# Sparse attention, a routed expert layer and a second expert layer in one kernel: a front in another order, a placement step in bf16, two weight chunks ahead instead of three, and row transposes spaced by VectorE's backlog

## The chip, the core and the metric

The kernel runs on one core of a Trainium2 chip. The metric is the device time of one execution in microseconds, from start to end of the program. A profiled execution also has a span, the time from its first to its last instruction. TensorE (PE in the profile) does the matmuls and transposes, VectorE (DVE), ScalarE (ACT) and GpSimd (POOL) the elementwise work, and SyncE (SP) and GpSimd start the DMA transfers.

## What is computed

```python
# q, k, v: (4, 8, 576, 64); heads 0-3 attend locally (0 <= i-j < 32), heads 4-7 with stride 32
scores = scale * q @ k.T;  attn = softmax(where(mask, scores, -1e9));  attn_out = attn @ v
x = attn_out.transpose(0, 2, 1, 3).reshape(2304, 512)
# first layer: 8 experts (512 -> 1024 -> 512), at most 288 tokens each
logits = x @ w_gate;  order = argsort(-logits.flatten())   # greedy assignment in this order
for e in range(8):  out[assigned == e] = relu(x[assigned == e] @ w1[e]) @ w2[e]
# second layer: 4 experts, all tokens, weighted by p = domain_probs / sum
out2 = sum(p[:, e:e+1] * (relu(out @ v1[e]) @ v2[e]) for e in range(4))
```

## The kernel before, in words

The whole program is one instruction stream for each engine, written in Python in the order in which each engine runs it. An engine waits at an instruction until its operands are there, and everything behind it on that engine waits with it.

**The front** (`front`) does the attention of the four batches. A batch is 10 units: five strided units (two groups of 6 or 7 row pairs, heads 4 to 7) and then five local ones (heads 0 to 3). The loop over `t` is a software pipeline. In step `t` unit `t` gets its scores (`scores`, L186 strided and L189 local, with the mask and row minimum on VectorE, L196), unit `t-1` its exponentials on ScalarE (`exps`, L205), unit `t-2` its division on GpSimd (`norm`, L215), unit `t-4` the transposes of its probabilities (`tr_p`, L222, copied to `pT`), and unit `t-5` the product with v (`av`, L235 or L242, copied to `hold`). Beside these, each of eight steps of a batch (`t` mod 10 from 6 to 9 and from 0 to 3) prepares two of the 16 pieces of q and k of the next batch (`pre` calls `piece`). Four strided pieces each of q and k are four transposes of 72 columns (L153). Four local pieces each of q and k are six matmuls with the identity, each of 64 output rows and 96 columns, which the trace shows as 12 instructions (L164). A piece's copy out of PSUM goes to ScalarE or VectorE: `copy` gives "q" pieces to the two in turn by a counter of all copies, strided k pieces to ScalarE and local k pieces to VectorE. Batch 0's pieces are done ahead of the loop (the first eight) and in its first steps.

Loads of q, k and v are issued on SP's queue: for batch `b+2` q and k, and for batch `b+1` v, in step 2 of batch `b`. The strided part of v (`vs`) is 13 transfers a batch, of 18 to 126 rows of 512 bytes. Local q and k (`ql`, `kl`) come in pieces of 1536 contiguous bytes, the local part of v (`vl`) in pieces of 256.

**Routing and the first expert.** Behind the last unit, `search` finds the first expert's tokens, and `place` turns them into a list of row numbers: 18 bf16 matmuls (L708) give a small table `tk`, copied to f32, and three f32 matmuls of it with `rad` (L714, six instructions in the trace, as each f32 matmul is two) give `idx`. GpSimd gathers the rows of x by `idx` (`xg`, L902, three indirect DMAs), PE transposes them (L926), ScalarE and VectorE split them into high and low halves (`xh`, `xl`), and the first expert's matmuls (`l1`, L982) begin. Meanwhile `PRE` = 3 chunks of expert weights are loaded and split (a chunk is two transfers `raw` of 256 KB on SP, L829 and L830; the cast `wh` on ScalarE, L855; the rest `wl` on VectorE or GpSimd). PE runs `WAIT` = 16 matmuls on constants (L1329) while it waits for the rows.

**The experts.** PE then runs the chunks of both layers. Each product is three matmuls (high by high, high by low, low by high). The search, placement and gather of expert `g+1` are two generators that hand out work between the matmuls. `Pace` keeps a running estimate of PE's and VectorE's time in the program's order (`nc.pe`, `nc.dve`), and a `yield` says when the generator goes on. For experts 1 to 7 the gathered rows are transposed in four groups of three (L919), each into the one PSUM buffer `pb`; a group can start only when the split of the group before has been read out of it (`xh` on ScalarE, then `xl` on VectorE). The groups stand 1.8 us of the estimate apart.

Of the kernel before, what the change touches and what calls it, by code (L numbers as in the profile page):

```python
# [18 lines left out]
FT = mybir.dt.float32  # L19
# [10 lines left out]
WARM = 10  # L30
WAIT = 16
BUSY = (0, 8, 2)
MORE = (1, 1, 5, 1, 1, 1, 1, 1)

def dap(t, off, *dims):
    return bass.AP(tensor=t.tensor, offset=t.offset + off, ap=[list(d) for d in dims])

def front(tc, ident, hot, q, k, v, wg, dp, xd, L, ready, hold, deferred):
# [3 lines left out]
    with ExitStack() as st:  # L42
# [8 lines left out]
        def load_qk(b, kinds="sl"):  # L51
            T = LD.setdefault(b, {})
            if "s" in kinds:
                for nm in ("qs", "ks"):
                    T[nm] = ld.tile([72, 32, 64], FT, name=nm)
            n = 8 if b == 0 else 32
            for r in range(0, 32 if "s" in kinds else 0, n):
                for nm, src in (("qs", q), ("ks", k)):
                    nc.sync.dma_start(T[nm][:, r:r + n].rearrange("p r d -> p (r d)"), dap(src, (b * H + 4) * hs + r * D, [hs, 4], [32 * D, 18], [1, n * D]))
            for nm, src in (("ql", q), ("kl", k)) if "l" in kinds else ():  # L60
                T[nm] = ld.tile([96, 4, 6, 64], FT, name=nm)
                nc.sync.dma_start(T[nm].rearrange("p h r d -> p h (r d)"), dap(src, b * H * hs, [6 * D, 96], [hs, 4], [1, 6 * D]))

        def load_v(b, lo=0, hi=10):
            T = LD[b]
            if not lo:
                T["vs"] = ld.tile([126, 10, 128], FT, name="vs")
            for t, (b0, n) in list(enumerate(zip(starts, sizes)))[lo:hi]:
                p = 0
                while p < n:  # L70
                    h, rp = divmod(b0 + p, 16)
                    m = min(n - p, 16 - rp)
                    nc.sync.dma_start(T["vs"][18 * p:18 * (p + m), t], dap(v, (b * H + 4 + h) * hs + 2 * rp * D, [2 * D, m], [32 * D, 18], [1, 2 * D]))
                    p += m
# [11 lines left out]
        load_qk(1, "s")  # L86
        load_v(0, 6)
        load_qk(1, "l")
        load_vl(0)
        zero = cst.tile([128, 128], FT, name="zero")  # L90
# [51 lines left out]
        def piece(b, i):  # L142
# [12 lines left out]
            else:  # L155
# [5 lines left out]
                src, dst = LD[b][("ql", "kl")[j]], (QL, KL)[j][b]  # L161
                for t in range(3):
                    for x in range(2):
                        nc.tensor.matmul(p[64 * x:64 * x + 64, 96 * t:96 * t + 96], src[:, 2 * hp + x, 3 * a + t, :], ident[:96, :96], start=True, stop=True)  # L164
                copy(dst[:, hp, 32 * j:].rearrange("p (s a t) -> p a t s", a=2, t=3)[:, a], p[:, :288].rearrange("p (t s) -> p t s", t=3), sc, "q" if sc else "r")

# [207 lines left out]
        for t in range(N + 14):  # L374
            t_now[0] = t
            if t < N and t % 10 == 2 and units[t][0] + 1 < B:
                if units[t][0] + 2 < B:
                    load_qk(units[t][0] + 2)
                load_v(units[t][0] + 1)
                nxt = [(units[t][0] + 1, i) for i in ORDER]  # L380

# [16 lines left out]
            def at(d, f):  # L398
                if 0 <= t - d < N:
                    f(t - d)  # L400
# [21 lines left out]
            while late:  # L422
                late.pop(0)()
            if t == N + 4:
                logits(N - 1)
            at(5, av)
            rows("o")
            if t < N:
                at(10, logits)
            elif t == N + 3:  # L430
                logits(N - 3)
            elif t == N + 5:
                logits_local(N - 1)
            pre()
            at(1, exps)
            rows("s")
            if t < N:
                scores(t)
            pre()
        for x in late2 + late:  # L440
# [15 lines left out]
def route_consts(nc, cst):  # L456
    K = {}
# [49 lines left out]
    nc.gpsimd.affine_select(rsel, radix, pattern=[[-2, 3], [-6, 3], [-1, 2]], base=0, channel_multiplier=1, compare_op=OP.is_equal, fill=0.0)  # L507
    K["rad"] = cst.tile([128, 3, 3], FT, name="rad")
    nc.vector.tensor_reduce(K["rad"], rsel, AX.X, OP.add)
    K["first"] = [cst.tile([128, NC], FT, name="m0"), cst.tile([128, NC], FT, name="mw0"), cst.tile([128, NC + 3, 32], BF, name="oh0"),  # L510
# [173 lines left out]
def place(nc, K, wk, ps, out):  # L684
# [8 lines left out]
    if "W" not in K:  # L693
        K["W"] = wk.tile([128, NC * 18 + 110], BF, name="W")
        nc.gpsimd.memset(K["W"][:, NC * 18:], 0.0)
        K["tk"] = wk.tile([128, 224], FT, name="tk")
        nc.gpsimd.memset(K["tk"], 0.0)
# [32 lines left out]
HI = 2.0  # L730
PRE = 3

# [28 lines left out]
def experts(tc, ident, hot, K, L, xd, side, w1, w2, v1, v2, out, hold, deferred):  # L761
    nc = Pace(tc.nc)
    D, F = 512, 1024
    with ExitStack() as st:
# [126 lines left out]
        def chain_b():  # L891
            nt = 0
            for g in range(8):
# [21 lines left out]
                if g:  # L915
                    for dc in range(4):
                        p = ps.tile([128, 3, 96], FT, name="pb")
                        for k in range(3):
                            nc.tensor.transpose(p[:, k], xg[:, k, cs(dc)], ident[:96, :96])  # L919
                        split(X[0][:, dc], X[1][:, dc], p.rearrange("p k s -> p (k s)"), False)  # L920
                        yield 1.8
                else:
# [396 lines left out]

        loads(1, 3)  # L1320
        until(lambda: "gather" in R[0])
# [74 lines left out]
```

## Time and profile before

| | |
|---|---|
| time, median of 3 runs | 1187.33 us (1186.92 to 1189.51) |
| profiled execution | 1188.98 us, span 1187.3 us |
| PE busy | 1160.4 us, 98% of the span |
| DVE, ACT, POOL busy | 840.5, 618.6, 412.2 us |
| front, first score matmul to the last units | 12 to 124 us of the span |
| search and placement of the first expert | 124 to 146 us |
| first expert matmul | 154.5 us |

Busy time of PE counts overlapping and pipelined matmuls, so a stretch that is 98% busy can still hold work that takes longer than it must. The clock granted to TensorE is 1.00 when it runs at 2.4 GHz and 0.50 at 1.2 GHz.

### The profile page before, as it was taken

How to read it: one execution, taken by the hardware profiler on the slowest of the kernel's cores; microseconds unless marked ns; L12 is line 12 of the kernel's file. 1: busy time of each engine (PE TensorE's matmuls, PEld its weight loads, DVE VectorE, ACT ScalarE, POOL GpSimd, SP SyncE). 2: the span in 40 equal slices, each digit the busy share in tenths (PEclk: the TensorE clock that was granted, in tenths of full speed). 3: DMA queues.
4: the chain of work that ended last, by engine and by line, in shares of the span. 5: the costliest groups of instructions: out<-in, count | busy, mean ns of one | idle time of the engine just before them, and what ended most of it. 6: DMA issues, size and time to landing. Idle time of an engine off the chain costs nothing.

```text
span 1187.3 us, 24963 instructions
## 1 busy us (share of the span) xinstructions
PE 1160.4 (98%) x9088; PEld 1038.2 (87%) x9095; DVE 840.5 (71%) x2249; ACT 618.6 (52%) x1602; POOL 412.2 (35%) x456
## 2 busy tenths in 40 slices
PE   9999799999999999999999999999999999999997
PEld 5777588898898988899999999999898999899996
DVE  6777687787785877878765577777777776766663
ACT  5899455442442442555545455555555555555552
POOL 4333030000010001001012566565666556766553
PEclk9999899999999999999999999999999999999999
DMA  8772574553353442566665433333433333433320
GB/s 181 170 172 44 151 222 145 178 169 102 90 163 91 134 154 58 160 213 185 191 199 158 128 107 91 105 104 95 140 100 96 107 94 102 142 92 105 102 77 36
DMA packets 191955, 152.98 MB, mean 129 GB/s; under 512 B 27640, under 2 KB 158776, under 8 KB 191400
## 3 DMA queue, kind: packets, MB, share of 16 engines
q1 hardware_dynamic: 188664, 141.74, 41.1%
q0 software_dynamic: 3168, 9.65, 2.6%
q8 instruction: 71, 1.16, 0.4%
q14 instruction: 52, 0.43, 0.1%
HBM read 141.77 MB, written 9.58 MB: 127 GB/s over the span
## 4 chain that ended last, share of the span: by engine, by line
PE 83%; DVE 5%; DMA 4%; issue 3%; POOL 3%; ACT 2%; SPq 0%; POOLq 0%; DVEq 0%; ACTq 0%
PE o L982 36%; PE h L982 17%; PE h L1214 9%; PE pa L1214 7%; DMA raw<-in_moe_w_dram 3%; PE pb L1214 3%; PE tr L164 2%; DVE wl L757 2%; PE pt L222 2%; POOL wl L1201 1%; PE av L242 1%; PE s L186 1%; PE pa L608 1%; PE tr L153 1%; PE av L235 1%
## 5 line engine op out<-in xcount | busy, mean ns | idle before, releaser
L757 DVE TENSOR_TENSOR wl<-raw,wh 128x512 fp32r<-128x512 f32 x352 | 269.2, 795 | 5.5 <-ACT wh L855 2.2
L875 ACT ACTIVATE hh<-h 128x256 fp32r<-128x256 f32 (+1 forms) x256 | 100.1, 391 | 273.4 <-PE h L982 201.4
L982 PE MATMUL o<-wh,hh 128*128 128x512 f32 x576 | 227.1, 394 | 0.4 <-DVE hold L757 0.4
L982 PE MATMUL o<-wl,hh 128*128 128x512 f32 x576 | 226.9, 394 | 0.0
L982 PE MATMUL o<-wh,hl 128*128 128x512 f32 x576 | 225.9, 392 | 0.0
L855 ACT CAST wh<-raw 128x512 fp32r<-128x512 f32 x272 | 160.4, 619 | 68.6 <-DMA raw<-in_moe_w_dram 67.0
L757 DVE SCALAR_TENSOR_TENSOR hl<-h,hh 128x256 fp32r<-128x256 f32 (+1 forms) x256 | 110.0, 430 | 118.0 <-ACT hh L875 117.4
L1201 POOL TENSOR_TENSOR wl<-raw,wh 128x512 fp32r<-128x512 f32 x96 | 122.3, 1295 | 197.1 <-ACT wh L1200 165.4
L902 POOL DMA_INDIRECT xg<-xd,idx x24 | 26.4, 1101 | 352.7 <-DVE idx L757 281.4
L982 PEld LDWEIGHTS o<-wh,hl 128*128 128x128 f32 x576 | 108.3, 188 | 22.8
L982 PEld LDWEIGHTS o<-wh,hh 128*128 128x128 f32 x576 | 108.3, 188 | 6.2 <-PE h L982 0.6
L982 PEld LDWEIGHTS o<-wl,hh 128*128 128x128 f32 x576 | 108.4, 188 | 5.5
L757 DVE TENSOR_TENSOR wl<-sums,wh 128x512 fp32r<-128x512 f32 x96 | 81.7, 852 | 29.0 <-ACT wh L1187 28.9
L1187 ACT CAST wh<-sums 128x512 fp32r<-128x512 f32 x96 | 59.7, 623 | 81.4 <-POOL sums L1175 57.8
L982 PE MATMUL h<-xh,wh 128*128 128x288 f32 x256 | 76.3, 298 | 0.0
L982 PE MATMUL h<-xl,wh 128*128 128x288 f32 x256 | 76.0, 297 | 0.0
L982 PE MATMUL o<-hh,wl 128*128 128x288 f32 x256 | 75.9, 297 | 0.0
L982 PE MATMUL o<-hl,wh 128*128 128x288 f32 x256 | 75.8, 296 | 0.0
L982 PE MATMUL o<-hh,wh 128*128 128x288 f32 x256 | 75.8, 296 | 0.0
L982 PE MATMUL h<-xh,wl 128*128 128x288 f32 x256 | 75.6, 295 | 0.0
L982 PE MATMUL h<-y256l,wh 128*128 128x256 f32 x256 | 73.0, 285 | 0.2 <-DVE y256l L757 0.2
L982 PE MATMUL h<-y256h,wl 128*128 128x256 f32 x256 | 73.2, 286 | 0.0
(312 smaller groups left out, 2937.3 us busy)
## 6 DMA issues: line engine op xcount, KB each, us to landing
raw<-in_moe_w_dram SPq DMA_DIRECT2D x464, 256.0 KB
vl<-in_v_dram SPq DMA_DIRECT2D x16, 192.0 KB
ql<-in_q_dram SPq DMA_DIRECT2D x4, 576.0 KB
kl<-in_k_dram SPq DMA_DIRECT2D x4, 576.0 KB
qs<-in_q_dram SPq DMA_DIRECT2D x3, 576.0 KB
ks<-in_k_dram SPq DMA_DIRECT2D x3, 576.0 KB
xd<-y SPq DMA_DIRECT2D x2, 576.0 KB
xd<-hl SPq DMA_DIRECT2D x5, 192.0 KB
```

What stands on the lines that cost most here:

```text
L153: nc.tensor.transpose(p[:, 72 * a:72 * a + 72], src[:, r:r + 2, :].rearrange("p r d -> p (r d)"), ident[:72, :72])
L164: nc.tensor.matmul(p[64 * x:64 * x + 64, 96 * t:96 * t + 96], src[:, 2 * hp + x, 3 * a + t, :], ident[:96, :96], start=True, stop=True)
L186: nc.tensor.matmul(out[:rows], lt, rt, start=True, stop=True)
L222: nc.tensor.transpose(p[:keys, rows * j:rows * j + rows], T["p"][:rows, j, :keys], ident[:rows, :rows])
L757: return f(*args, **kw)
L855: nc.scalar.copy(c["h"][:, sl], c["raw"][a])
L875: nc.scalar.activation(hi, src, AF.Relu)
L902: nc.gpsimd.indirect_dma_start(out=xg[:, k, :], out_offset=None, in_=xd, in_offset=bass.IndirectOffsetOnAxis(ap=idx[:, k:k + 1], axis=0))
L982: nc.tensor.matmul(out, a, b, start=start, stop=stop)
L1187: nc.scalar.copy(S["W"][nm][0], src[nm]())
L1201: nc.gpsimd.tensor_tensor(l, r, h.bitcast(FT), OP.subtract)
L1214: mmx = lambda o, a, b, first, lastm, n: (nc.tensor.matmul(o, a, b, start=first, stop=lastm, skip_group_check=True), tick(n / 2315 + 0.009))
```

## The change

The change does these things, beside two constants:

- In the front, local q and k of batches 1 to 3 come with the four heads side by side (8 transfers a batch in place of 2, pieces of 256 bytes in place of 1536), so that a piece is three transposes of 128 rows and 96 columns in place of six matmuls (12 instructions). The copy of a local piece walks the same elements in another order: three neighbours at a time.
- Inside a step, the two pieces and the exponentials come first, then `logits` and `av`, and the scores last.
- For batches 1 to 3 the last five of the ten `vs` tiles (six transfers a batch) are issued on GpSimd. Loads are put in another order, and batch 1's strided q and k come in two halves.
- `rad` and `tk` are bf16, so that each product of L714 is one bf16 matmul.
- `PRE` is 2 and `WAIT` 13.
- For experts 1 to 7, the groups of row transposes stand as far apart as VectorE's estimated backlog and 0.6 us, at least 1.8 us.

```diff
-WAIT = 16
+WAIT = 13
...
             for nm, src in (("ql", q), ("kl", k)) if "l" in kinds else ():
...
+                T[nm] = ld.tile([96, 6, 4, 64], FT, name=nm)
+                for h in range(4):
+                    nc.sync.dma_start(T[nm][:, :, h, :], dap(src, (b * H + h) * hs, [6 * D, 96], [D, 6], [1, D]))
...
-                    nc.sync.dma_start(T["vs"][18 * p:18 * (p + m), t], dap(v, (b * H + 4 + h) * hs + 2 * rp * D, [2 * D, m], [32 * D, 18], [1, 2 * D]))
+                    (nc.gpsimd if b and t > 4 else nc.sync).dma_start(T["vs"][18 * p:18 * (p + m), t], dap(v, (b * H + 4 + h) * hs + 2 * rp * D, [2 * D, m], [32 * D, 18], [1, 2 * D]))
...
                 for t in range(3):
+                    if b:
+                        nc.tensor.transpose(p[:, 96 * t:96 * t + 96], src[:, 3 * a + t, 2 * hp:2 * hp + 2, :].rearrange("p h d -> p (h d)"), ident[:96, :96])
+                        continue
                     for x in range(2):
                         nc.tensor.matmul(p[64 * x:64 * x + 64, 96 * t:96 * t + 96], src[:, 2 * hp + x, 3 * a + t, :], ident[:96, :96], start=True, stop=True)
-                copy(dst[:, hp, 32 * j:].rearrange("p (s a t) -> p a t s", a=2, t=3)[:, a], p[:, :288].rearrange("p (t s) -> p t s", t=3), sc, "q" if sc else "r")
+                copy(dst[:, hp, 32 * j:].rearrange("p (s a t) -> p a s t", a=2, t=3)[:, a], p[:, :288].rearrange("p (t s) -> p s t", t=3), sc, "q" if sc else "r")
...
-            if t == N + 4:
-                logits(N - 1)
-            at(5, av)
             rows("o")
+            pre()
+            at(1, exps)
+            rows("s")
+            pre()
             if t < N:
                 at(10, logits)
...
-            pre()
-            at(1, exps)
-            rows("s")
+            at(5, av)
             if t < N:
                 scores(t)
-            pre()
...
-        K["tk"] = wk.tile([128, 224], FT, name="tk")
+        K["tk"] = wk.tile([128, 224], BF, name="tk")
...
-PRE = 3
+PRE = 2
...
                         split(X[0][:, dc], X[1][:, dc], p.rearrange("p k s -> p (k s)"), False)
-                        yield 1.8
+                        yield max(1.8, nc.dve + 0.6 - nc.pe)
```

The rows below are the instructions of an engine in the order in which it runs them, before and with the change. The change has more lines of code, so that its line numbers are higher by 5 to 12: L222 is L230 in it, L164 is L169, L215 is L223, L829 is L841.

PE at the start of batch 2 (step `t` = 20; `tr` is the PSUM tile of a piece, `s` of scores, `av` of the product with v), before:

```order
L222 MATMUL pt<-ident,pr 96x128 x4
L340 MATMUL xr<-four,lg 128x16
L345 MATMUL xr<-four,lg 32x16
L242 MATMUL av<-pT,vl 64x64 x8
L164 MATMUL tr<-ident,ql 64x96 x6
L186 MATMUL s<-kS,qS 126x126 x4
L164 MATMUL tr<-ident,ql 64x96 x6
```

The same step with the change:

```order
L230 MATMUL pt<-ident,pr 96x128 x4
L348 MATMUL xr<-four,lg 128x16
L353 MATMUL xr<-four,lg 32x16
L169 MATMUL tr<-ident,ql 128x96 x6
L250 MATMUL av<-pT,vl 64x64 x8
L194 MATMUL s<-kS,qS 126x126 x4
```

Two groups of six matmuls on either side of the scores have become one group of six transposes (two pieces of three) ahead of `av`.

GpSimd around the turn from the local units of batch 0 to the strided ones of batch 1 (`pr` are probabilities divided by their sums, in place), before:

```order
L215 TENSOR_TENSOR pr<-pr,r 128x4x96 x4
L215 TENSOR_TENSOR pr<-pr,r 128x2x96
L160 MEMSET kL 128x2x32
L215 TENSOR_TENSOR pr<-pr,r 126x4x126 x2
L215 TENSOR_TENSOR pr<-pr,r 108x4x108 x2
```

With the change:

```order
L223 TENSOR_TENSOR pr<-pr,r 128x4x96 x4
L223 TENSOR_TENSOR pr<-pr,r 128x2x96
L165 MEMSET kL 128x2x32
L78 DMA vs<-in_v_dram 108x1x128 x2
L78 DMA vs<-in_v_dram 36x1x128
L78 DMA vs<-in_v_dram 72x1x128
L78 DMA vs<-in_v_dram 108x1x128 x2
L223 TENSOR_TENSOR pr<-pr,r 126x4x126 x2
```

Six transfers of `vs` now stand between the division of the last local unit and that of the first strided unit, here and at the same place of batch 1; those for batch 1 stand ahead of the first division of all.

SP at the first expert (`raw` are weights, `side` takes a copy of the gathered rows' last columns and so waits for the gather), before:

```order
L843 TENSOR_LOAD ei_2625
L843 ISA x2
L829 ISA
L829 DMA raw<-in_moe_w_dram 128x4x128
L830 ISA
L830 DMA raw<-in_moe_w_dram 128x512
L829 ISA
L829 DMA raw<-in_moe_w_dram 128x4x128
L830 ISA
L830 DMA raw<-in_moe_w_dram 128x512
L829 ISA
L829 DMA raw<-in_moe_w_dram 128x4x128
```

With the change, from the second chunk on:

```order
L841 DMA raw<-in_moe_w_dram 128x4x128
L842 ISA
L842 DMA raw<-in_moe_w_dram 128x512
L918 DMA side<-xg 96x3x8
L841 ISA
L841 DMA raw<-in_moe_w_dram 128x4x128
L842 ISA
L842 DMA raw<-in_moe_w_dram 128x512
```

The third chunk's two loads now stand behind `side`. On ScalarE, before and then with the change (`hh` is the high half of the first matmuls' result, read out of PSUM):

```order
L855 CAST wh<-raw 128x512 x6
L879 CAST xh<-o 128x288 x4
L875 ACTIVATE hh<-h 128x288
L855 CAST wh<-raw 128x512 x2
L875 ACTIVATE hh<-h 128x288
```

```order
L867 CAST wh<-raw 128x512 x4
L891 CAST xh<-o 128x288 x4
L867 CAST wh<-raw 128x512 x2
L887 ACTIVATE hh<-h 128x288
L867 CAST wh<-raw 128x512 x2
```

The casts of the third chunk stand behind the rows' casts and ahead of the first `hh`.

## Rows read from the trace of the kernel before

**Rows 1.** The page, part 1: busy time, share of the span and instructions of each engine.

```profile
PE 1160.4 (98%) x9088; PEld 1038.2 (87%) x9095; DVE 840.5 (71%) x2249; ACT 618.6 (52%) x1602; POOL 412.2 (35%) x456
```

**Rows 2.** Busy time by stretch: length; PE, PEld, DVE, ACT, POOL; clock, DMA share, GB/s.

```profile
34.97:49.30 14.33, 14.33 (x222) 11.10 (x223) 10.35 (x51) 11.57 (x52) 4.06 (x6) 1.00 0.81 187
51.18:63.78 12.60, 12.60 (x206) 9.63 (x205) 10.36 (x72) 11.67 (x55) 4.88 (x7) 1.00 0.81 190
63.78:75.64 11.86, 11.86 (x214) 9.87 (x212) 9.08 (x53) 10.34 (x46) 3.75 (x5) 1.00 0.73 172
...
89.43:101.18 11.75, 11.75 (x213) 9.76 (x211) 9.27 (x53) 11.28 (x51) 4.15 (x6) 1.00 0.53 105
...
141.40:151.60 10.20, 7.52 (x38) 3.86 (x39) 5.42 (x19) 3.09 (x5) 4.20 (x4) 0.50 0.76 230
...
98.00:100.00 2.00, 2.00 (x44) 1.58 (x43) 1.18 (x11) 2.00 (x11) 0.75 (x2) 1.00 1.15 162
```

**Rows 3.** The chain that ended last, 64 to 92 us: start, length, what.

```profile
65.30 0.50 PE tr L164 x12
...
66.43 0.65 PE tr L164 x12
...
80.42 0.40 PE tr L153 x4
```

**Rows 4.** Groups of ScalarE instructions up to 125 us: busy time, mean ns, idle before.

```profile
L136 ACT ACTIVATE qL<-tr 128x288 f32<-128x288 f32 x7 | 4.8, 684 | 4.4 <-PE tr L164 4.2
...
L136 ACT ACTIVATE qS<-tr 128x288 f32<-128x288 f32 x11 | 4.5, 413 | 6.5 <-PE tr L153 6.3
```

**Rows 5.** All engines in order of time, 64 to 77 us: start, length, instruction, [idle, releaser].

```profile
71.72 1.29 POOL L215 TENSOR_TENSOR pr<-pr,r 126x504 f32<-126x504 f32 x1 [2.74 <-ACT hold L134]
...
75.64 0.65 PE L222 MATMUL pt<-ident,pr 126*126 126x126 f32 x4
```

**Rows 6.** GpSimd in order of time, 0 to 140 us.

```profile
10.66 0.57 POOL L119 DMA_DIRECT2D dpr<-in_moe_domain_probs_dram  x1
...
86.51 1.23 POOL L393 DMA_DIRECT2D xd<-side  x1 [1.85 <-DVE r L214]
```

**Rows 7.** All engines in order of time, 140 to 160 us.

```profile
143.38 0.45 SPq L829 DMA_DIRECT2D raw<-in_moe_w_dram  x1
...
144.86 1.44 PE L714 MATMUL pb<-rad,tk 128*128 128x3 f32 x6 [0.34 <-DVE tk L757]
...
146.34 0.16 DVE L757 CAST idx<-pb 96x3 int32<-96x3 f32 x1 [1.53 <-PE pb L714]
...
146.44 1.28 ACT L855 CAST wh<-raw 128x512 fp32r<-128x512 f32 x2 [7.33 <-DMA raw<-in_moe_w_dram]
...
154.07 0.38 SPq L829 DMA_DIRECT2D raw<-in_moe_w_dram  x1
...
154.51 0.48 PE L982 MATMUL h<-xh,wh 128*128 128x288 f32 x1
...
156.55 0.41 ACT L875 ACTIVATE hh<-h 128x288 fp32r<-128x288 f32 x1 [1.46 <-PE h L982]
...
158.16 0.41 ACT L875 ACTIVATE hh<-h 128x288 fp32r<-128x288 f32 x1
```

**Rows 8.** The chain that ended last, 158 to 660 us: its shares by line.

```profile
by line: PE h L982 38.7%; PE o L982 37.6%; DMA raw<-in_moe_w_dram 7.2%; DVE wl L757 3.2%; PE pa L608 2.1%; ACT wh L855 1.5%; issue 1.4%; PE pb L919 1.2%; DVE G L757 1.1%; DVE hl L757 1.1%; ACT hh L875 0.7%; PE pb L714 0.7%; PE pb L708 0.5%;
```

**Rows 9.** Waits of PE over the whole span: total us, times, longest.

```profile
PE pb L919 <- DVE xl L757: 5.9, 6, 2.0
```

**Rows 10.** All engines in order of time, 218 to 232 us.

```profile
226.34 1.25 ACT L855 CAST wh<-raw 128x512 fp32r<-128x512 f32 x2 [2.34 <-DMA raw<-in_moe_w_dram]
...
227.50 0.39 ACT L879 CAST xh<-pb 128x288 fp32r<-128x288 f32 x1
...
228.44 0.47 PE L919 MATMUL pb<-ident,xg 96*128 96x96 f32 x3 [1.77 <-DVE xl L757]
```

**Rows 11.** PE in order of time, 426 to 434 us.

```profile
432.86 0.47 PE L919 MATMUL pb<-ident,xg 96*128 96x96 f32 x3 [1.96 <-DVE xl L757]
```

More of the change, by code (lines that the diff above doesn't have):

```diff
@@ L55, in load_qk @@
                     T[nm] = ld.tile([72, 32, 64], FT, name=nm)
-            n = 8 if b == 0 else 32
+            n = 8 if b == 0 else 16 if b == 1 else 32
             for r in range(0, 32 if "s" in kinds else 0, n):
@@ L60, in load_qk @@
             for nm, src in (("ql", q), ("kl", k)) if "l" in kinds else ():
-                T[nm] = ld.tile([96, 4, 6, 64], FT, name=nm)
-                nc.sync.dma_start(T[nm].rearrange("p h r d -> p h (r d)"), dap(src, b * H * hs, [6 * D, 96], [hs, 4], [1, 6 * D]))
+                if b == 0:
+                    T[nm] = ld.tile([96, 4, 6, 64], FT, name=nm)
+                    nc.sync.dma_start(T[nm].rearrange("p h r d -> p h (r d)"), dap(src, b * H * hs, [6 * D, 96], [hs, 4], [1, 6 * D]))
+                    continue
+                T[nm] = ld.tile([96, 6, 4, 64], FT, name=nm)
+                for h in range(4):
+                    nc.sync.dma_start(T[nm][:, :, h, :], dap(src, (b * H + h) * hs, [6 * D, 96], [D, 6], [1, D]))
         def load_v(b, lo=0, hi=10):
@@ L87, in front @@
         load_v(0, 6)
+        load_vl(0)
         load_qk(1, "l")
-        load_vl(0)
         zero = cst.tile([128, 128], FT, name="zero")
@@ L162, in piece @@
                 for t in range(3):
+                    if b:
+                        nc.tensor.transpose(p[:, 96 * t:96 * t + 96], src[:, 3 * a + t, 2 * hp:2 * hp + 2, :].rearrange("p h d -> p (h d)"), ident[:96, :96])
+                        continue
                     for x in range(2):
                         nc.tensor.matmul(p[64 * x:64 * x + 64, 96 * t:96 * t + 96], src[:, 2 * hp + x, 3 * a + t, :], ident[:96, :96], start=True, stop=True)
-                copy(dst[:, hp, 32 * j:].rearrange("p (s a t) -> p a t s", a=2, t=3)[:, a], p[:, :288].rearrange("p (t s) -> p t s", t=3), sc, "q" if sc else "r")
+                copy(dst[:, hp, 32 * j:].rearrange("p (s a t) -> p a s t", a=2, t=3)[:, a], p[:, :288].rearrange("p (t s) -> p s t", t=3), sc, "q" if sc else "r")
         def shape(n):
@@ L377, in front @@
                 if units[t][0] + 2 < B:
-                    load_qk(units[t][0] + 2)
+                    load_qk(units[t][0] + 2, "s")
                 load_v(units[t][0] + 1)
+                if units[t][0] + 2 < B:
+                    load_qk(units[t][0] + 2, "l")
                 nxt = [(units[t][0] + 1, i) for i in ORDER]
@@ L431, in front @@
                 logits(N - 3)
+            elif t == N + 4:
+                logits(N - 1)
             elif t == N + 5:
                 logits_local(N - 1)
-            pre()
-            at(1, exps)
-            rows("s")
+            at(5, av)
             if t < N:
                 scores(t)
-            pre()
         for x in late2 + late:
@@ L507, in route_consts @@
     nc.gpsimd.affine_select(rsel, radix, pattern=[[-2, 3], [-6, 3], [-1, 2]], base=0, channel_multiplier=1, compare_op=OP.is_equal, fill=0.0)
-    K["rad"] = cst.tile([128, 3, 3], FT, name="rad")
-    nc.vector.tensor_reduce(K["rad"], rsel, AX.X, OP.add)
+    radf = cst.tile([128, 3, 3], FT, name="radf")
+    nc.vector.tensor_reduce(radf, rsel, AX.X, OP.add)
+    K["rad"] = cst.tile([128, 3, 3], BF, name="rad")
+    nc.vector.tensor_copy(K["rad"], radf)
     K["first"] = [cst.tile([128, NC], FT, name="m0"), cst.tile([128, NC], FT, name="mw0"), cst.tile([128, NC + 3, 32], BF, name="oh0"),
@@ L1318, in fast @@
                 f()
-        loads(1, 3)
+        loads(1, PRE)
         until(lambda: "gather" in R[0])
```

## The prediction

> **What bounds the kernel now.** I read the busy times first: PE is busy 98% of the span [rows 1], so a gain has to be PE time or a wait of PE. Then the front by stretch, cut at the steps in which local pieces are prepared (10 to 13, 20 to 23, 30 to 33) [rows 2]. PE is busy throughout them at clock 1.00, but ScalarE is close behind: 11.57 us of 14.33, 10.34 of 11.86, 11.28 of 11.75. In the five steps between the first two (51.18 to 63.78) ScalarE has 11.67 of 12.60. So PE work that is saved counts only until ScalarE is the limit, and that comes soonest in batch 3. The chain shows PE pieces end to end there: two local pieces a step, 0.50 and 0.65 us, and a strided piece 0.40 [rows 3]. Then the way to the first expert: from 141.4 to 151.6 us the clock is 0.50, that is 1.2 GHz, with PE busy 7.52 of 10.20 us [rows 2]; `idx` comes at 146.34 and the first expert matmul at 154.51 [rows 7]. Last, the experts: of PE's waits 5.9 us, in six pieces, are the row transposes waiting for `xl` [rows 9].
>
> **The front.** A new piece is three transposes of 96 columns, 288 columns in all; a strided piece is four of 72, also 288. At 0.40 a piece two cost 0.80 where two now cost 1.15: 0.35 saved a step. The other end is a quarter of the instructions, 3 for 12, at a quarter of the time: 0.86. Standing side by side should save a little over the first, so I take 0.45, nearest to the strided row. Twelve steps give 5.4 us (4.2 to 10.3). ScalarE's spare time caps it by batch: 2.76, 1.52 and 0.47 us [rows 2]. The new order of the copies may lift the cap: `qL` takes 684 ns on ScalarE for the same 288 elements that `qS` writes in 413 [rows 4]; `qL` writes single elements apart, `qS` runs of 18, the new copy runs of 3, so between 0 and 0.27 us a copy, of which I take one a batch in batch 3. That is 1.8 + 1.5 + 0.7 = 4.0 us. The scores' new place at the end of a step leaves ScalarE the copies of the pieces and `pT` to do while VectorE makes the minima, so I charge nothing; if ScalarE has no copy at hand it waits for VectorE, which would eat the same spare time. Which pieces ScalarE copies shifts by three `qS` out of 11, 1.2 us off its total; they lie in other steps, and I count nothing.
>
> The six `vs` transfers on GpSimd stand ahead of the first strided division. GpSimd is free from 71.72 - 2.74 = 68.98 and does that division at 71.72 for 1.29 us [rows 5]; PE wants the result at 75.64 [rows 5], in the change some 1.5 us sooner, 74.1. A plain DMA of one piece a partition held GpSimd for 0.57 us, one of many small pieces 1.23 [rows 6]. Six by 0.57 end at 72.4 and the division at 73.7: in time. Six by 1.23 end at 76.4 and the division at 77.7: PE, and behind it every step, 3.6 us late. The `vs` transfers have one piece a partition, so the first row is nearer; I take 0.5 us. The other such turn lies behind a stretch 2.5 us longer [rows 2], so it has room. In batch 0 the transfers run before GpSimd has any division. The 256-byte pieces of `ql` and `kl` cost DMA time: while `vl`, of such pieces, was moved at 98 to 100 us, the DMA was full at 162 GB/s [rows 2], so 1.18 MB a batch take 7.3 us. They are issued eight steps, over 20 us, ahead of use, which hides it; without that cover up to 7.3 us would show. In batch 1 the cover is thinnest, since they are now behind `vl`. Front: -4.0 + 0.5 = -3.5 us.
>
> On GpSimd's DMAs the Trainium skill (SBUF — State Buffer, "SBUF: two separate sides") speaks against the change: while VectorE runs an instruction that takes the port pair it shares with GpSimd, GpSimd cannot write descriptors, and a DMA of 620 ns took 3100. By that price the six would take 18.6 us in place of 3.4, at each of two turns. The trace agrees with no such factor: 1.23 us is its longest here, with VectorE at work.
>
> **The first expert.** L714 starts at 144.86 and `idx` follows 1.48 us later, with six instructions in 1.44 us, 0.24 each [rows 7], at 1.2 GHz. Three bf16 products remain. Bounds: the same price each saves 0.7; the price of the L708 products (below), doubled for the clock, saves 1.3. L708 is the nearest, being bf16 with the same 128 columns of weights; I take 1.1. The gather is issued that much sooner, and so the first matmul: 153.41. The three constant matmuls fewer cost nothing as long as PE waits for the rows anyway; they matter only if the clock then stays at 1.2 GHz into the first products, which 3 us longer would price at 1.5.
>
> Against it, the third chunk's loads now stand behind the copy that waits for the gather. SP's next load after that copy was at 154.07 [rows 7], so 152.97 now. The first load of all, into an idle DMA, was issued at 143.38 and cast at 146.44: 3.06 us. That gives a cast at 156.0, the second load's some 0.6 later, 0.64 each: the casts end at 157.25. Only then does ScalarE reach the first `hh` (0.41 us, [rows 7]), and VectorE's half after it takes about as long: 158.1. The third product needs that PSUM buffer and this chunk. Products were 1.61 apart (156.55 and 158.16, [rows 7]), so it was due at 153.41 + 3.22 = 156.6. PE waits 1.5 us (0 if the loads take half, 2.5 if the DMA is shared). First expert: -1.1 + 1.5 = +0.4 us.
>
> **The placement of the other seven.** Of the chain between 158 and 660 us (502 us) L714 holds 0.7% and L708 0.5% [rows 8]: 3.5 us and 2.5, for seven experts 0.50 each and 0.36 each. The 18 products of L708 thus cost 0.02 each. Three in place of 0.50 save 0.44, by seven 3.1 us (1.7 if only the number is halved, 3.5 at most). PE does nothing else then, so all of it counts.
>
> **The row transposes.** The two longest of the six waits are 1.77 us (expert 1, third group, [rows 10]) and 1.96 (expert 4, third group, [rows 11]). The order of the changed program puts 24 matmuls in place of 11 between expert 4's second and third groups, over 2 us more work: that wait goes. Expert 1's third group stands about 1.2 us later behind its first: 0.6 stays, because what is late there is ScalarE's cast, which sat 2.34 us behind a weight load [rows 10] that VectorE's backlog knows nothing of. Expert 5's groups stand as before, and keep 0.45; the three smaller ones go. With 0.65 for new waits, my choice, 1.7 are left: -4.2 us (-1.9 if the two longest stay, -5.9 if all go).
>
> **Sum.** -3.5 + 0.4 - 3.1 - 4.2 = -10.4 us on a span of 1187.3. The profiled execution was 1.7 us above its span and as much above the median of the runs; the median is 1187.33, so the forecast is **1177.0 us**.
>
> **The rivals.** *The front gives nothing*: ScalarE stays the limit, or the divisions come 3.6 us late, or batch 1's loads do. For it speaks ScalarE's 96% in batch 3 [rows 2]; against it the 2.8 us spare in batch 1. The front then lies between -0.4 and +3: 1180 to 1183.5. *The backlog rule misses its waits*: the two longest come from a cast behind a load. 2.3 us less: 1179.3. *All of it pays*: no chunk wait, transposes at the lower price: a front of -6 and -1.1 for the first expert, 1172. *The clock*: fewer plain matmuls in the local steps, and the clock falls there to 1.2 GHz as it did at 141.4 for 10.2 us. One such stretch costs 5.1, three 15.3: 1182 to 1192. Against it: the strided steps, whose pieces are transposes already, keep clock 1.00 (51.18 to 63.78, [rows 2]). *Slower*: GpSimd's DMAs get through only once a step, 2.97 us each (11.86 by four). Six take 17.8 us, the division ends at 88.1, 14 us late, and 11.5 at the other turn: 1177 - 0.5 + 25.5 = 1202. It decides from 1.95 us a transfer on, where the kernel is 0.2% slower. That is the rule of the SBUF page, and 1.23 [rows 6] is the most that the trace shows.
>
> **How the numbers follow.** The forecast as told (1174 to 1180) 0.47, the front gives nothing 0.20, the rule misses 0.12, all of it pays 0.12, the clock 0.04, slower 0.05. From 1171 to 1185.5 holds the first three and most of the fourth, the clock's cheapest case too: a little over 8 in 10. A change under 0.2%, 2.4 us, is about what a measurement of this kernel cannot tell from none: below 1184.9 is faster, above 1189.7 slower. Faster 0.88 (the first four but for a tenth of the second, and a part of the clock), same 0.05, slower 0.07.
>
> **What would show it.** In the changed profile the local steps should be 0.3 to 0.5 us shorter and ScalarE the fuller engine in them; `pt` should not wait for `pr` at steps 14 and 24; L714 should fall to some 0.1 us and `idx` come 1.1 us after the table's copy starts or sooner; PE should wait 1.5 us before its third product; L919 should keep under 2 us of waits. I am wrong if GpSimd's DMAs last over 1.2 us, if the clock falls in the front, or if the experts' saved waits return as waits for weights.

## The result, and the profile after

| | before | after |
|---|---|---|
| time, median | 1187.47 us (4 runs, 1186.92 to 1189.51) | 1176.88 us (4 runs, 1176.55 to 1177.56) |
| ratio | | 0.9908 (95% interval 0.9891 to 0.9926) |
| profiled execution, its span | 1188.98, 1187.3 us | 1176.97, 1175.3 us |

The forecast was 1177.0 us. The median fell by 10.6; the span fell by 12.0, since the profiled execution of before lay 1.5 us above its median. To see where they came from, I follow five stations on the path through both traces: the start of the last probabilities' transposes (`pt`), of L714 (L726 now), of the fifth and of the last `hh` on ScalarE, and the end of the span.

| station, us | before | after | difference | gained or lost on the way | forecast |
|---|---|---|---|---|---|
| last `pt` | 117.62 | 110.71 | -6.91 | -6.9 (front) | -3.5 |
| L714, first expert | 144.86 | 138.02 | -6.84 | +0.1 | 0 |
| fifth `hh` | 167.67 | 161.99 | -5.68 | +1.2 (first expert) | +0.4 |
| last `hh` | 1174.90 | 1161.42 | -13.48 | -7.8 (other experts) | -7.3 |
| end | 1187.3 | 1175.3 | -12.0 | +1.5 (after the last work) | 0 |

So the total agrees better than its terms, and that is luck: the front gave twice what I had forecast, and two losses stand against that, one of which I had not thought of. Each station is read from one profile; in the control's (after_again below) the same four ways are -5.8, +0.1, +1.3 and -7.1, and the end is +1.5 again.

The page of after, part 1; then busy time by stretch, cut at the same steps as [rows 2] and at the strided steps between them:

```profile
PE 1146.8 (98%) x8845; PEld 1028.9 (88%) x8852; DVE 837.7 (71%) x2253; ACT 613.7 (52%) x1599; POOL 424.3 (36%) x474
```

```profile
core 0: us, PE busy (x) PEld busy (x) DVE busy (x) ACT busy (x) POOL busy (x), PEclk, DMA share, GB/s
33.52:45.05 11.53, 11.02 (x155) 9.40 (x151) 8.73 (x48) 9.71 (x45) 6.82 (x12) 1.00 0.82 189
45.05:60.02 14.97, 14.31 (x229) 11.10 (x227) 10.40 (x79) 14.69 (x68) 6.04 (x8) 1.00 0.86 185
60.02:70.04 10.02, 9.93 (x143) 8.17 (x139) 8.39 (x48) 9.13 (x43) 6.17 (x10) 1.00 0.73 191
...
84.26:94.44 10.18, 9.86 (x142) 8.09 (x139) 8.10 (x51) 9.30 (x42) 3.99 (x6) 1.00 0.60 118
```

The local stretches [rows 2] fell from 14.33, 11.86 and 11.75 to 11.53, 10.02 and 10.18 us: 2.8, 1.8 and 1.6 shorter. (The first takes 10.80 to 12.24 us in the seven kernels with this front, so it is known to 0.7 us either way; the two others agree within 0.1.) ScalarE still has 1.8, 0.9 and 0.9 us to spare in them, though they fell by all of its spare time of before and more: it was no cap. The strided stretch between the first two is 0.5 us longer (14.48 before, from 49.30 to 63.78 us), with ScalarE now busy 14.69 of 14.97.

The way through the first expert in after, all engines in order of time, which answers to [rows 7]:

```profile
138.02 0.24 PE L726 MATMUL pb<-rad,tk 128*128 128x3 bf16 x3 [0.34 <-DVE tk L769]
...
138.30 0.16 DVE L769 CAST idx<-pb 96x3 int32<-96x3 f32 x1 [0.34 <-PE pb L726]
...
145.03 0.55 PE L938 MATMUL o<-ident,xg 96*128 96x96 f32 x4 [1.01 <-DMA xg<-xd,idx]
...
145.58 0.38 SPq L841 DMA_DIRECT2D raw<-in_moe_w_dram  x1
...
148.46 1.32 ACT L867 CAST wh<-raw 128x512 fp32r<-128x512 f32 x2 [1.78 <-DMA raw<-in_moe_w_dram]
...
149.68 0.40 ACT L887 ACTIVATE hh<-h 128x288 fp32r<-128x288 f32 x1
...
150.63 0.40 PE L994 MATMUL h<-xh,wh 128*128 128x288 f32 x1 [1.02 <-DVE hl L769]
...
151.73 0.40 PE L994 MATMUL h<-xh,wl 128*128 128x288 f32 x1 [0.56 <-DVE wl L769]
```

Read it as a chain: SP issues the third chunk at 145.58, ScalarE stands 1.78 us until it is there, casts it, and only then writes the first `hh`; VectorE's half follows, and PE waits 1.02 and 0.56 us, 1.58 in all for the 1.5 of the forecast. What the forecast did not have is what comes behind that wait (busy time by stretch):

```profile
150.00:152.00 2.00, 0.81 (x4) 0.57 (x5) 1.88 (x3) 0.38 (x2) 1.12 (x1) 1.00 1.04 340
152.00:154.00 2.00, 2.00 (x13) 2.00 (x13) 1.14 (x3) 1.77 (x4) 0.86 (x1) 0.73 1.05 338
154.00:158.00 4.00, 4.00 (x25) 3.92 (x24) 3.98 (x4) 2.10 (x4) 3.34 (x3) 0.71 0.81 260
```

PE was busy 0.81 of 2.00 us; then the clock fell to 0.50 (1.2 GHz) from 152.92 to 156.33 us, which before had stayed at 1.00 from 151.51 on. It costs up to half of these 3.41 us.

PE's waits in the experts, 158 to 1165 us, the four longest (total us, times, longest), against [rows 9]:

```profile
PE pa L1226 <- ACT u L1264: 1.6, 2, 0.8
PE pb L931 <- DVE xl L769: 1.2, 1, 1.2
PE pa L620 <- DVE G L769: 0.7, 1, 0.7
PE o L994 <- DVE hold L769: 0.5, 1, 0.5
```

The row transposes (L931) wait 1.2 us, once, where L919 waited 5.9 in six pieces; it is expert 1's third group, the one that the forecast said would stay.

### The profile page after: what moved, and what is told of

Read it like the earlier page. It is cut to its first block, busy times and chain, and to the rows that moved or that the text cites. A ratio compares the mean times of both kernels' runs of the same rounds, so it can differ in the third digit from the quotient of the medians.

```text
span 1175.3 us, 24533 instructions
## 1 busy us (share of the span) xinstructions
PE 1146.8 (98%) x8845; PEld 1028.9 (88%) x8852; DVE 837.7 (71%) x2253; ACT 613.7 (52%) x1599; POOL 424.3 (36%) x474
## 4 chain that ended last, share of the span: by engine, by line
PE 85%; ACT 4%; POOL 3%; DVE 3%; issue 3%; DMA 2%; POOLq 0%; SPq 0%; DVEq 0%; ACTq 0%
PE o L994 38%; PE h L994 19%; PE h L1226 9%; PE pa L1226 7%; PE pb L1226 3%; ACT pr L213 2%; DMA raw<-in_moe_w_dram 1%; POOL wl L1213 1%; PE pa L620 1%; PE pt L230 1%; POOL out_dram L1090 1%; DVE wl L769 1%; PE s L194 1%; PE av L250 1%; ACT pT L139 1%
## 5 line engine op out<-in xcount | busy, mean ns | idle before, releaser
L994 PE MATMUL o<-hh,wh 128*128 128x288 f32 x256 | 76.7, 300 | 0.0
```

The costliest lines, as they stand in the source:

```text
L994: nc.tensor.matmul(out, a, b, start=start, stop=stop)
```

## The experiments

All are compared with the kernel before, run beside them on the same chip, where its median was 1189.6 (the four on the front), 1188.8 (yield18 to early3) and 1189.1 us (the rest). The control, after_again, is the changed kernel itself; "to control" is the difference of the medians. The control ran beside the last group, on another chip than the first eight, so for these "to control" holds to about 1 us: their ratios less that of the control, by 1189 us, give +7.4, +3.4, -1.3, -0.2, +4.4, +5.5, +2.0 and +2.3. No run undoes `WAIT` or the order of the loads by itself.

| kernel | median us (lowest to highest) | ratio to before (95%) | to control |
|---|---|---|---|
| after_again | 1178.43 (1177.01 to 1179.16) | 0.9903 (0.9883 to 0.9922) | |
| old_front | 1186.22 (1185.17 to 1188.31) | 0.9965 (0.9949 to 0.9981) | +7.8 |
| old_pieces | 1182.74 (1181.70 to 1183.98) | 0.9932 (0.9905 to 0.9959) | +4.3 |
| old_step | 1178.08 (1177.18 to 1178.42) | 0.9892 (0.9865 to 0.9918) | -0.4 |
| old_copy | 1179.35 (1177.82 to 1181.71) | 0.9901 (0.9873 to 0.9928) | +0.9 |
| yield18 | 1182.52 (1181.07 to 1182.79) | 0.9940 (0.9927 to 0.9954) | +4.1 |
| f32_rad | 1183.01 (1181.82 to 1183.78) | 0.9949 (0.9935 to 0.9962) | +4.6 |
| pre3 | 1179.55 (1177.13 to 1179.76) | 0.9920 (0.9907 to 0.9934) | +1.1 |
| early3 | 1179.56 (1179.05 to 1180.95) | 0.9922 (0.9909 to 0.9936) | +1.1 |
| vs_on_sp | 1179.94 (1175.05 to 1183.73) | 0.9921 (0.9897 to 0.9945) | +1.5 |
| gate3 | 1176.75 (1176.17 to 1177.34) | 0.9894 (0.9874 to 0.9913) | -1.7 |
| gate3_mix | 1176.17 (1175.90 to 1177.88) | 0.9893 (0.9873 to 0.9913) | -2.3 |

**after_again**: no edit.

> The changed kernel itself, once more, as the control for the other kernels: the kernel before came out 1 to 2 us longer beside the last eight kernels (1189.6 and 1188.8) than beside the changed kernel (1187.5). If that is the chip, the changed kernel is longer here too, 1178 to 1179, at an unchanged ratio of 0.991 to the kernel before, and three chunks ahead (0.992) are worth nothing or cost 1 us. If it stays at 1176.9, three chunks ahead cost 2.7 us.

Its ratio is that of the first measurement, so the longer times here are the chip's, and three chunks ahead (0.992) gain nothing.

**old_front**: the function `front` as it stood before; all else as changed.

> The changed kernel with the front as it was before (pieces, loads, order inside a step, v's transfers); all else as changed. The traces of the two kernels say that the front's last transposes come 6.9 us sooner with the change, so this theory expects 1176.9 + 6.9 = 1183.8 us. By the sum of the forecast the front is worth 3.5: 1180.4 us. The rival that the front gives nothing, because what it saves is lost in the search and the gather behind it, expects 1177.

The ratio says +6.8 us (0.9965 - 0.9908 by 1189), the medians 7.8. That this is near the 6.9 of the first table is in part chance. In its own trace, the slowest of its twelve runs (2.1 us above the median), the way from step 4 to the last `pt` is 6.7 us longer than in after (97.40 and 90.71), the end 1.5 shorter, for a reason told below, and the experts, whose code is that of after, are 5.7 longer. There PE waits once for ScalarE's copy `y`, with a stretch of 3.41 us at half clock behind it:

```profile
PE o L984 <- ACT y L1062: 1.8, 1, 1.8
```

So the front with its price at the end is worth some 5.2 us by the traces: more than the 3.5 of the forecast, and not nothing. The rest of the 7.8 lies in the experts.

**old_pieces**:

```diff
-                    if b:
-                        nc.tensor.transpose(p[:, 96 * t:96 * t + 96], src[:, 3 * a + t, 2 * hp:2 * hp + 2, :].rearrange("p h d -> p (h d)"), ident[:96, :96])
-                        continue
                     for x in range(2):
-                        nc.tensor.matmul(p[64 * x:64 * x + 64, 96 * t:96 * t + 96], src[:, 2 * hp + x, 3 * a + t, :], ident[:96, :96], start=True, stop=True)
+                        nc.tensor.matmul(p[64 * x:64 * x + 64, 96 * t:96 * t + 96], (src[:, 3 * a + t, 2 * hp + x, :] if b else src[:, 2 * hp + x, 3 * a + t, :]), ident[:96, :96], start=True, stop=True)
```

> The changed kernel, but a local piece of batches 1 to 3 is again six matmuls (12 instructions) instead of three transposes; layout, loads, order of the step and order of the copies stay as changed. If the transposes alone made the front shorter, the three local stretches (11.53, 10.02 and 10.18 us) go back to about 14.3, 11.9 and 11.8, some 6 us, of which the strided stretches give back up to 0.9: 1182 to 1183 us. By the forecast's term 4.0: 1180.9. If it was the order of the step that made room, little comes back: under 1179.

The same stretches of old_pieces, by its own steps:

```profile
33.43:46.64 13.21, 13.21 (x226) 11.16 (x223) 9.05 (x48) 10.91 (x49) 7.46 (x12) 1.00 0.79 185
...
61.48:72.66 11.18, 11.18 (x214) 9.86 (x210) 8.99 (x51) 9.56 (x45) 6.61 (x11) 1.00 0.74 164
...
86.72:97.90 11.18, 11.18 (x214) 9.86 (x210) 8.30 (x51) 9.57 (x43) 4.11 (x6) 1.00 0.41 69
```

They are 1.68, 1.16 and 1.00 us longer than in after, 3.8 in all, of which the strided stretches give back 0.3 (the first with the spread told above), and the run 4.3. So the transposes are worth about what the forecast gave the whole front (4.0), but the stretches do not go back to 14.3, 11.9 and 11.8: another 1.1, 0.7 and 0.6 us come from the rest of the front.

**old_step**: the order inside a step as before.

> The changed kernel with the old order inside a step of the front: the product with v first, then a piece, the exponentials, the scores, and the second piece last. The forecast charged the order with nothing: 1176.4 to 1177.4 us. The rival is that the order, with the scores at the end of the step, is what lets TensorE run without waits now that the pieces are short: 1179 or more, with waits of TensorE for the maxima and copies in the local steps.

```profile
35.08:46.38 11.30, 11.30 (x151) 9.26 (x152) 9.05 (x46) 10.45 (x49) 7.00 (x12) 1.00 0.77 183
46.38:60.80 14.42, 14.42 (x229) 10.94 (x227) 12.26 (x85) 13.51 (x64) 6.23 (x8) 1.00 0.94 215
```

The forecast's zero is right as a sum, and from batch 1 on the old order is the shorter one. The 11.30 for 11.53 says nothing, since that stretch varies by more; but the strided stretch is back at 14.42, where nine profiles with the new order and the new pieces have 14.97 to 14.99. So the new order made it longer. From step 10 to the last `pt` it costs 1.2 us (77.19 in after, 75.98 here), and it gains 0.7 in batch 0 (13.52 from step 4 to step 10, 14.22 here).

**old_copy**:

```diff
-                copy(dst[:, hp, 32 * j:].rearrange("p (s a t) -> p a s t", a=2, t=3)[:, a], p[:, :288].rearrange("p (t s) -> p s t", t=3), sc, "q" if sc else "r")
+                copy(dst[:, hp, 32 * j:].rearrange("p (s a t) -> p a t s", a=2, t=3)[:, a], p[:, :288].rearrange("p (t s) -> p t s", t=3), sc, "q" if sc else "r")
```

> The changed kernel, but the copy of a local piece writes single elements apart again, as before. A qL copy on ScalarE then goes from 468 back to some 684 ns and a kL copy on VectorE from 446 to 671. ScalarE has 1.82, 0.89 and 0.88 us to spare in the local stretches now, and five such copies cost 1.1 in all: nothing to 0.5 us shows, 1176.9 to 1177.4. The rival is that ScalarE's spare time is an average and the copies stand in TensorE's way one for one: 1.1 us and more, 1178 to 1180.

The copies of a local piece on ScalarE and VectorE (busy time, mean ns), first in after, then in old_copy:

```profile
L141 ACT ACTIVATE qL<-tr 128x288 f32<-128x288 f32 x5 | 2.3, 468 | 0.0
...
L143 DVE COPY kL<-tr 128x288 f32<-128x288 f32 x12 | 4.8, 446 | 0.0
```

```profile
L141 ACT ACTIVATE qL<-tr 128x288 f32<-128x288 f32 x5 | 3.4, 684 | 0.0
...
L143 DVE COPY kL<-tr 128x288 f32<-128x288 f32 x12 | 7.2, 675 | 0.0
```

The three local stretches of old_copy are 12.27, 10.23 and 10.69 us, 1.5 more than after:

```profile
34.09:46.36 12.27, 11.46 (x154) 9.43 (x151) 10.04 (x48) 10.08 (x45) 7.21 (x12) 1.00 0.82 187
...
61.34:71.57 10.23, 10.00 (x143) 8.16 (x139) 8.79 (x50) 9.46 (x43) 6.17 (x10) 1.00 0.68 168
...
85.91:96.60 10.69, 10.01 (x142) 8.11 (x138) 9.17 (x51) 9.83 (x43) 4.03 (x6) 1.00 0.49 97
```

0.6 of the 1.5 is PE waiting for batch 1's `ql` and `kl`, loads that it waits for in the control too. That leaves 0.9, as the medians say (the ratios say -0.2), at an interval that holds zero. So the sizes of a copy are as expected, and the rival (spare time on ScalarE is an average) is the nearer one by the medians, the expectation by the ratios: it is not settled.

**yield18**: `yield 1.8` for `yield max(1.8, nc.dve + 0.6 - nc.pe)`.

> The changed kernel with the groups of row transposes 1.8 us apart again, whatever VectorE's backlog is. The forecast's term: 4.2 us back, 1181.1. By the traces the waits of those transposes fell from 5.9 to 1.2 us, so 4.7 back: 1181.6. The rival is that the waits were only moved (TensorE now waits at other places instead): 1 to 2 us, 1178 to 1179, and the waits for h, G and y fall by as much as those of the transposes rise.

PE's waits in its experts, the two longest:

```profile
PE pb L931 <- DVE xl L769: 3.6, 4, 1.5
PE o L994 <- ACT y L1072: 2.5, 1, 2.5
```

The time is as forecast, the way to it only half: the row transposes wait 3.6 us, 2.4 more than in after, and at 343.60 us a product waits 2.5 us for ScalarE's copy `y` (0.4 in after), with a stretch of 3.41 us at half clock behind it. In the kernel before, with the same 1.8, no wait of PE for `y` reaches 0.15 us: that half belongs to this combination of parts, not to the rule alone.

**f32_rad**: `rad` and `tk` in f32 again.

> The changed kernel with the small table and the radix weights in f32 again, so that each of the three products is two instructions. Forecast: 1.1 us for the first expert, whose gather comes that much later, and 0.44 for each of the seven others, 4.2 in all: 1181.1 us. The rival is that for the seven others TensorE's extra time is hidden and only the first expert's shows: 1178. If the first expert's gain was eaten by the third weight chunk, 3.1: 1180.

4.6 us for 4.2. L726 has 48 instructions of 252 ns (median) where the changed kernel has 24 of 164. One of the seven later placements and what PE runs next, in f32_rad and in after:

```profile
206.53 0.73 PE L726 MATMUL pb<-rad,tk 128*128 128x3 f32 x6
...
207.12 0.48 PE L994 MATMUL o<-wl,hh 128*128 128x512 f32 x1
```

```profile
204.63 0.23 PE L726 MATMUL pb<-rad,tk 128*128 128x3 bf16 x3
...
204.72 0.48 PE L994 MATMUL o<-wl,hh 128*128 128x512 f32 x1
```

The next product starts 0.59 us behind L726 in place of 0.09, and at the six other placements it is the same: 0.49 each, 3.4 in all, where the forecast had 0.44 and 3.1. The first expert's `idx` comes 1.48 us behind L726 as before, not 0.28: 1.2 more.

**pre3** and **early3**: `PRE = 3`; and `loads(1, 3)` in place of `loads(1, PRE)` with `PRE` still 2.

> The changed kernel with three weight chunks ahead of the first expert's rows again. The forecast charged the late third chunk with 1.5 us: 1175.4. The trace of the changed kernel shows 1.58 us of waits before the third product and behind them a stretch of 3.41 us at half clock, which costs up to 1.7 more: up to 3.3 us, and some 0.4 back because the rows land later beside the third chunk's transfers: 1174 to 1174.5. The rival is that the third chunk's transfers and casts ahead of the rows cost as much as they save: 1176.5 to 1177.5.

> The changed kernel with the third chunk's two transfers issued ahead of the first expert's rows, but its casts left where the change put them, behind the rows' split. If what costs is that the transfers stand behind the copy that waits for the gather, this gains as much as three whole chunks ahead or a little more, since the casts and halves do not stand before the rows' split: 1173.6 to 1174.5 us. If the transfers' share of the DMA delays the rows by as much, 1176.5 to 1177.5.

Neither gains (1.1 us longer than the control by the medians, 2.0 and 2.3 by the ratios). PE's first row transpose in pre3 and in early3:

```profile
144.91 2.15 PE L938 MATMUL o<-ident,xg 96*128 96x96 f32 x12 [2.62 <-ACT wh L867]
```

```profile
145.36 2.15 PE L938 MATMUL o<-ident,xg 96*128 96x96 f32 x12 [2.53 <-DMA xg<-xd,idx]
```

| us | first load | `idx` | first row transpose | first product | fifth `hh` | fifth `hh` behind `idx` |
|---|---|---|---|---|---|---|
| before | 143.38 | 146.34 | 152.28 | 154.51 | 167.67 | 21.3 |
| after | 136.27 | 138.30 | 143.16 | 146.09 | 161.99 | 23.7 |
| pre3 | 135.44 | 137.56 | 144.91 | 148.19 | 160.96 | 23.4 |
| early3 | 136.04 | 138.15 | 145.36 | 148.65 | 163.66 | 25.5 |
| gate3 | 135.59 | 137.60 | 142.87 | 145.28 | 160.03 | 22.4 |

With three chunks ahead the row transposes begin 8.9 to 9.5 us behind the first load (before, pre3, early3), whether `idx` comes 2.96 us behind it or 2.12: the rows wait for DMA time. In pre3 the profile names ScalarE's sixth cast, which ends at 144.90 and had itself waited for the third chunk; in early3, where that cast stands behind the rows, it names the rows. With two chunks the first transposes come 6.9 us behind the first load, the last third of the rows 8.8. So the rival holds: what three chunks save behind the rows they cost ahead of them, and PE then runs the transposes and constants at half clock (0.73 on the mean of 146 to 150 us in pre3).

**gate3**:

```diff
                 if g == 0:
+                    gate = wk.tile([1, 8], FT, name="gate")
+                    nc.gpsimd.memset(gate, 0.0)
+                    nc.sync.dma_start(K["gd"], gate)
+                    loads(PRE + 1, 0)
                     nc.sync.dma_start(dap(side, 0, [8, 96], [96 * 8, 3], [1, 8]), xg[:, :, 512:])
```

> The changed kernel, with the third chunk's two transfers on SyncE's queue released when GpSimd has issued the last of the first expert's three gathers (SyncE first writes eight numbers that GpSimd sets behind the gathers), in place of when the rows have landed: 2 us sooner, but behind the rows in the DMA queues. If the late third chunk costs what the trace shows, and only the shared DMA gave it back when the transfers went ahead, the waits of 1.02 and 0.56 us and the half-clock stretch go: 1.6 to 3.3 us faster than the control. If the transfers still delay the third group of rows, or the clock falls anyway, 0 to 1 us.

All engines of gate3 in order of time:

```profile
141.56 0.09 POOL L919 MEMSET gate<- 1x8 f32 x1
141.68 0.31 SPq L920 DMA_DIRECT2D gd<-gate  x1
...
142.19 0.39 SPq L841 DMA_DIRECT2D raw<-in_moe_w_dram  x1
...
145.73 1.17 ACT L867 CAST wh<-raw 128x512 fp32r<-128x512 f32 x2
...
147.31 0.41 ACT L887 ACTIVATE hh<-h 128x288 fp32r<-128x288 f32 x1 [0.41 <-PE h L998]
```

The third chunk is issued 4.6 us behind `idx` in place of 7.3, its cast waits for nothing, the first `hh` waits for PE and not PE for it; the two waits are gone, and the clock stays at 1.00 from 142.34 us to the end of the experts. The fifth `hh` comes 1.3 us sooner behind `idx`, and the median is 1.7 lower (by the ratios 1.1). That is the low end of what was expected: ahead of the fifth `hh` PE now waits 1.6 us for `G` (L620, the search), which it does not in after. The kernel has the shorter time of the two in all but the overlap of 0.3 us between its slowest run and the control's fastest; its ratio's interval still holds the control's.

**gate3_mix**: gate3, with the old order in a step from `t` = 10 on.

> The same, and the order inside a step of the front is the new one in batch 0's ten steps and the old one from then on. In the traces the new order is 0.7 us shorter in batch 0 and the old one 1.2 us shorter over the rest: 1.2 us faster than the kernel with the gate alone. If that difference was noise between profiled executions, no difference.

From step 10 to the last `pt` it takes 76.0 us where gate3 takes 76.7; the medians differ by 0.6, and the runs of both overlap. A gain of half a microsecond is likely and not shown. It is the fastest of all by its median.

**vs_on_sp**: `nc.sync` for all `vs`.

> The changed kernel with all strided v transfers on SyncE's queue, none on GpSimd. The forecast charged GpSimd's transfers with 0.5 us, since the first division might come late: 0.5 us faster than the control. The trace of the changed kernel shows them at 0.63 us each with no division late: no difference. If loads behind them on SyncE's queue then come later, up to 1 us slower.

The runs spread over 8.7 us, where the control's spread over 2.2. The profiled execution is the fastest, so what made the others late is not seen. It shows something else: the last line of the program, where each engine drains, on GpSimd's queue; first in after, then in vs_on_sp (durations in ns, min/median/max):

```profile
L1403 POOLq DRAIN  x3: 46/98/6590, 1167.9 to 1175.0; - x3
```

```profile
L1403 POOLq DRAIN  x3: 46/98/5122, 1167.4 to 1173.1; - x3
```

That is the 1.5 us at the end: from the last `hh` on it takes 12.37 us in vs_on_sp and before, 13.84 in after.

## Why the forecast held, point by point

- **The front, -3.5 for -6.9: the step that failed.** "ScalarE's spare time caps it by batch" is wrong. The three stretches fell by 2.80, 1.84 and 1.57 us, past the caps of 2.76, 1.52 and 0.47, and ScalarE did not become the fuller engine in them (9.71 us to PE's 11.02 of 11.53). The shorter copies, of which I had counted one, in batch 3 alone, are not the whole reason: in old_copy, with copies as long as before, the stretches of batches 2 and 3 still fell by 1.6 and 1.1 us. What I had wrong: ScalarE's work is not tied to the stretch. Its busy time in the three fell by 5.05 us; the five `qL` copies are 1.1 of that, and 2.5 came back in the two strided stretches between them. These were, before:

```profile
49.30:63.78 14.48, 14.48 (x228) 10.99 (x227) 11.87 (x80) 12.81 (x59) 5.45 (x7) 1.00 0.75 176
...
75.64:89.43 13.79, 13.61 (x224) 10.49 (x223) 10.83 (x79) 12.79 (x57) 6.63 (x10) 1.00 0.65 147
```

And after (the first of them, 14.69 of 14.97, is shown further up):

```profile
70.04:84.26 14.22, 13.44 (x223) 10.52 (x223) 12.21 (x87) 13.45 (x64) 7.64 (x11) 1.00 0.94 203
```

- **What the front is made of.** The transposes themselves: 0.45 a step forecast, 0.32 measured (3.8 us by 12), or 0.50 read from one step alone (two pieces in 0.65 us of PE, at 60.88 to 61.53, for 1.15). "I charge nothing" for the scores' place holds as a sum. Of the 6.9, 0.7 lies ahead of step 4, which the profiles of kernels with this front reach between 19.28 and 20.58 us (20.74 before): that is no gain of the front. Of the 6.2 behind it (5.7 to 7.0 in the seven profiles) 3.8 is the transposes and about 0.9 the copies; the new order gives 0.7 in batch 0 and takes 1.2 behind it. The rest, about 2 us, shows only with several parts together.
- **GpSimd's six transfers, +0.5: 0.2 at most at that turn, and 1.5 at the end, which I had put at nothing.** They took 0.63 us each (604 to 672 ns, 18 of them), the first row of [rows 6] and not the second. The six before batch 2's division end at 68.93, the division at 69.97, and PE begins `pt` at 70.04, 0.72 us behind the start of the scores ahead of it; in vs_on_sp, where GpSimd had done the division earlier, it is 0.56. The price is elsewhere: 18 more transfers make GpSimd's drain at the end 1.47 us longer (0.08 each). It is 6.59 in every profile with them and 5.12 in before, old_front and vs_on_sp.
- **On the port rule** (the Trainium skill, SBUF — State Buffer, "SBUF: two separate sides"; 620 ns alone, 3100 beside VectorE): the trace shows no such price. 672 ns was the longest, and VectorE was busy 3.69 of the 3.73 us from 65.20 to 68.93 in which six of them ran. The page gives its rule for some of VectorE's instructions, and no run here tells whether any of those beside the six are of that kind: the rule as such is neither shown nor refuted. The slower rival, which priced them at 2.97, falls.
- **"Issued eight steps, over 20 us, ahead of use" fails in batch 1.** There `ql` stands behind `vl` and is issued from 28.52 us on, 5.9 us ahead of its first piece at 34.43. In the profile of after that costs little, in the control's 1.2 us:

```profile
29.66 3.47 SPq L67 DMA_DIRECT2D ql<-in_q_dram  x4
...
37.10 0.44 PE L169 MATMUL tr<-ident,ql 96*128 96x96 f32 x3 [1.25 <-DMA ql<-in_q_dram]
```

- **The first expert, +0.4 for +1.2.** The terms were each right (`idx` 1.2 us sooner for 1.1; PE's wait 1.58 for 1.5), but they are not independent. With three chunks ahead the sooner `idx` would have gained nothing, for the rows wait for the chunks' transfers; the two chunks are what lets it count. f32_rad shows the other side: with two chunks ahead and a late `idx` the rows come 4.9 us behind `idx`, as in after. And behind the wait the clock fell, which I had considered only for the front and ahead of the first products.
- **The placement, -3.1, and idx: right.** 4.6 us measured for both, 4.2 forecast; by the trace 3.4 and 1.2.
- **The row transposes, -4.2: right in size** (4.1 in yield18), but there half by another wait, that for `y`, and that is luck. Their own waits fell by 4.7 from before to after.
- **The rivals.** The front giving nothing, the clock falling in the front (1.00 throughout, 33 to 94 us) and the rule missing its waits fell. "All of it pays" was right of the front and wrong of the chunk.
- **What does not add up.** Undone one at a time, front, rule and bf16 cost 16.5 us, the whole change 10.6. Some counts twice: yield18 and old_front each have a long wait for `y` and a half-clock stretch behind it, at 345 and 354 us, that neither before nor after has. The rest I cannot assign.

## What to carry to other kernels

An engine's spare time over a stretch is no cap on what another engine can gain there, since work can move into the next stretch: look at what each step waits for. A gather, and the loads that run ahead of it, share the DMA; here an index that came sooner gained only with fewer loads ahead of its rows (pre3), and a load that the gather released (gate3) came early without standing ahead of them. And follow the change to the last line of the program: what an engine must drain there counts in full.

## What the runs showed of the hardware

- GpSimd's final drain grew from 5.12 to 6.59 us with 18 more plain transfers on its queue, though the last of them was issued 1100 us earlier, and by the same amount in every kernel.
- Behind PE's two waits for the third chunk the clock went to 1.2 GHz for 3.41 us in after (1.02 and 0.56 us) and in the control (1.3 and 0.6), but not in vs_on_sp (1.2 and 0.6) nor in yield18 (1.7 and 0.6): the same wait may or may not cost the clock.
- The rows of the gather are on GpSimd's queue and the chunks on SP's, yet two more chunk transfers made the row transposes start 7.21 us behind `idx` in early3, where the profile names the rows, in place of 4.86 (7.35 in pre3, where it names a cast). A rule of the Trainium skill (DMA: Bandwidth & Descriptors, "Queues, rings and completion order") says that each DMA engine takes packets from the queues in turn; by it the rows get their share while the loads last, and the whole once they end. The table of the first expert does not speak against that; no run here shows the turns themselves.
- The same 288 elements out of PSUM took 684 ns on ScalarE and 675 on VectorE written one by one, and 468 and 446 in runs of three.
